# A recurrent memory transformer beside a routed expert: what is kept of each streamed weight block in SBUF

## The chip, the cores and the metric

The kernel runs on one core of one Trainium2 chip. The metric is the device time of one execution in microseconds. A core has a matrix engine (TensorE, PE in the profile, with its weight loads as PEld), VectorE (DVE), ScalarE (ACT), GpSimd (POOL), a sequencer that mostly issues DMAs (SyncE, SP), and sixteen DMA engines between HBM and the on-chip memory SBUF. Matmuls write to a second on-chip memory, PSUM.

## The reference

`x` is [2048, 1024] in bf16. It is normalised row by row; the result goes into two branches, and their sum and `x` are the output.

```
xn = layernorm(x)
out = x + A(xn) + B(xn)

# A: 64 segments of 32 rows, one after the other; 32 heads of 128, M = 8 memory rows
mem = mem0
for s in range(64):
    h = concat([mem, xn[32*s : 32*s+32]])          # 40 rows
    q, k, v = h @ Wq, h @ Wk, h @ Wv               # 1024 -> 32 heads x 128, each
    p = softmax(mask(q @ k.T * 128**-0.5))         # per head
    o = (p @ v) @ Wo                               # 4096 -> 1024
    mem = o[:8]
    outs.append(o[8:])

# B: the two rows with the largest xn @ w_r go through one gated expert
y = silu(xs @ w_gate) * (xs @ w_up) @ w_down       # 1024 -> 3584 -> 1024
B = xn, with y * sigmoid(r) added to the two rows
```

The memory rows of a segment come out of the segment before it, so the 64 segments run in sequence. Each one multiplies 40 rows by the four matrices Wq, Wk, Wv and Wo, 4 x 1024 x 4096 weights in bf16, 32 MB. SBUF does not hold all of that.

## The kernel before

**Granules.** The 32 MB of weights are cut into 64 granules of 128 x 2048 bf16: 512 KB, 4 KB in each of the 128 partitions. Granules 0 to 47 belong to Wq, Wk and Wv in the order of `PHASES` (six phases p of eight granules, kc = 0 to 7, each for half of the heads of one matrix); granules 48 to 63 belong to Wo, two heads each. A step is one segment and uses the granules in the order 0 to 63. One granule is four matmuls of 32 rows by 512 columns in the phases (L669, one for each quarter of 512 columns of the granule, into four partition groups of the accumulator `PSm`), and eight matmuls of 256 columns in the output projection (L730, into `WO`).

**Resident and streamed.** `streamed` (L75) lists 20 of the 64 granules, about every third; the other 44 are resident: loaded in the first step into a tile of their own (`load_resident`, L121, tiles `wres`) and kept. The streamed ones are loaded again in every step. In the first step they come from the input matrices, and GpSimd copies them once into contiguous DRAM tiles `wsc` (`copy_block`, L357), from which steps 1 to 63 read them (`fetch`, L327, issued by SP). They land in a pool of `N_SLOT` = 5 slots of 4 KB per partition (tile `g`). `after(s, g)` (L434) calls `fetch` whenever a streamed granule has been used, four granules ahead; in time, a load is issued when the matmuls of the granule that had its slot, five loads earlier, are done. SP issues its DMAs in program order.

**Two granules with other homes.** Granule 6 (`KEPT_WHOLE`) is held in PSUM, turned and turned back by `keep` (L334) in the first step, and brought into SBUF by `bring_back` (L348) in each later step: no load. Granule 25 (`KEPT_PART`) keeps its last two quarters in PSUM and streams the first two (`columns`, L107); `kept_piece` (L352) copies the two quarters from PSUM into the slot on VectorE in phase 2, after kc 1 and kc 2. So a step after the first has 19 loads, 18 of 512 KB and one of 256 KB.

**The rest of a step.** Small work is hung on places (p, kc) by `hook`: transposes of q and k (L516, copies QT on ACT and KT on DVE at kc 3 of the next phase), `scores` (L534, L536), `exponent` and `soften`, `attend` (L584, L586). A step ends with the cast of `WO` into `XN` (L791), whose memory rows feed the next step through two transposes (L259) and a copy into `ST` (L283). The memory rows' own outputs other than the recurrent ones ("left" rows, `left_pass` L647 into `PSl`, and `project` into `WL`) are computed for four segments together with the same granules while these are there. `after` also loads resident granules in the first step, 14 granules ahead, the last ten of them (whose tiles hold `x` before) from granule 44 on.

**The expert.** Its weights are 32 tiles of gate and up (448 KB each) and 14 of down (512 KB). In the last step `after` collects the tiles of used resident granules in `free_homes`, and `fetch_moe` (L371) loads into them; after the last step the five slots are added (L815), and all 46 loads have a place. Then come the choice of the two rows, 448 matmuls on gate and up (L873) and 112 on down (L886).

Of the kernel before, what the change touches and what calls it, by code (L numbers as in the profile page):

```python
# [8 lines left out]
BF16 = mybir.dt.bfloat16  # L9
# [5 lines left out]
PSUM = bass.MemoryType.PSUM  # L15
DRAM = bass.MemoryType.DRAM

N_RES = 44
N_SLOT = 5
KEPT_WHOLE = 6  # L20
KEPT_PART = 25
NEG = -30000.0

PHASES = [(0, 0), (1, 0), (0, 1), (1, 1), (2, 0), (2, 1)]
# [3 lines left out]
def kernel(  # L28
# [16 lines left out]
    nc = tc.nc  # L45
    P = 128
    Bsz, S, D = A_x.shape
# [7 lines left out]
    NT = S // P  # L55
# [16 lines left out]

    NG = 64

    streamed = [2, 5, KEPT_WHOLE, 9, 13, 17, 21, KEPT_PART, 29, 33, 36, 39, 42, 45, 47, 50, 53, 56, 59, 62]  # L75
    assert len(streamed) == NG - N_RES
    n_str = len(streamed)
    resident = [g for g in range(NG) if g not in streamed]

    def granule_dram(g):  # L80
        if g < 48:
            p, kc = divmod(g, KC)
            mat, half = PHASES[p]
            return Wqkv[mat][kc * P:(kc + 1) * P, 2048 * half:2048 * (half + 1)]
        w = g - 48
        return Wo2[2 * w * P:(2 * w + 2) * P, :].rearrange("(hh e) d -> e hh d", hh=2)

    def granule_out(t, g):
        return t[:, :] if g < 48 else t.rearrange("p (hh d) -> p hh d", hh=2)

    wres = ctx.enter_context(tc.tile_pool(name="wres", bufs=1))
    const = ctx.enter_context(tc.tile_pool(name="const", bufs=1))
    dram = ctx.enter_context(tc.tile_pool(name="dram", bufs=1, space=DRAM))
    front = ctx.enter_context(tc.tile_pool(name="front", bufs=1, reuse_waits="tile"))
    wstream = ctx.enter_context(tc.tile_pool(name="wstream", bufs=N_SLOT))
    one = ctx.enter_context(tc.tile_pool(name="one", bufs=1, reuse_waits="tile"))
# [7 lines left out]
    ql_d = [dram.tile([4, P, 512], BF16, name=f"ql_d{t}") for t in range(NT)]  # L104


    def columns(g, s):  # L107
        if s > 0 and g == KEPT_WHOLE:
            return None
        return slice(0, 1024 if s > 0 and g == KEPT_PART else 2048)  # L110

    wsc = {g: dram.tile([P, columns(g, 1).stop - columns(g, 1).start], BF16, name=f"wsc{g}")
           for g in streamed if g != KEPT_WHOLE}
    r_d = dram.tile([1, S], BF16, name="r_d")

# [2 lines left out]
    def home(g, shape, dtype, name):  # L118
        return wres.tile(shape, dtype, name=name, tag=f"wres{g}")
# [50 lines left out]
    for s in range(4):  # L170
        nc.vector.tensor_copy(out=SELM[:, s, 0:XM, :],
                              in_=IDENT[:, 32 * s:32 * s + XM].unsqueeze(2).to_broadcast([P, XM, 4]))
        nc.vector.tensor_copy(out=SELL[:, s, :, :],
                              in_=IDENT[:, 32 * s + XM:32 * s + SEG].unsqueeze(2).to_broadcast([P, XL, 4]))
# [129 lines left out]
    def new_stl(t):  # L304
# [7 lines left out]
    queued = []  # L312

    KEPT = [psK.tile([P, 1024], BF16, name=f"KEPT{b}") for b in range(3)]
    KEPT_COLS = {KEPT_WHOLE: {0: KEPT[0][:, 0:512], 1: KEPT[0][:, 512:1024], 2: KEPT[1][:, 0:512], 3: KEPT[1][:, 512:1024]},
                 KEPT_PART: {2: KEPT[2][:, 0:512], 3: KEPT[2][:, 512:1024]}}

    def fetch():
        if not flow:
            return  # L320
        s, g = flow.pop(0)
        t = wstream.tile([P, 2048], BF16, tag="g", name="g")
        c = columns(g, s)
        if s == 0:
            nc.sync.dma_start(out=granule_out(t, g), in_=granule_dram(g))
        elif c is not None:
            nc.sync.dma_start(out=t[:, c], in_=wsc[g][:, :])  # L327
        queued.append((g, t))

    def part(t, jq):  # L330
        return t[jq][:, :] if isinstance(t, list) else t[:, 512 * jq:512 * (jq + 1)]


    def keep(g, t):  # L334
        for c, K in KEPT_COLS[g].items():
            turned = PTB.rearrange("p (i r) -> p i r", i=4)
            for i in range(4):
                nc.tensor.transpose(out=turned[:, i, :], in_=t[:, 512 * c + P * i:512 * c + P * (i + 1)],
                                    identity=IDENT[:, :])
            XK = one.tile([P, 512], BF16, tag="vl", name="XK")  # L340
            nc.vector.tensor_copy(out=XK[:, :], in_=PTB)
            for i in range(4):
                nc.tensor.transpose(out=K[:, P * i:P * (i + 1)], in_=XK[:, P * i:P * (i + 1)], identity=IDENT[:, :])
# [7 lines left out]

    def kept_piece(g, c, copy):  # L352
        t = [t for q, t in queued if q == g][0]
        copy(out=t[:, 512 * c:512 * (c + 1)], in_=KEPT_COLS[g][c])  # L354


    def copy_block(g):  # L357
        c = columns(g, 1)
        if c is not None:
            src = granule_dram(g)  # L360
            nc.gpsimd.dma_start(out=granule_out(wsc[g], g), in_=src if g >= 48 else src[:, c])

    to_copy = list(streamed)
    flow += [(s, g) for s in range(NSEG) for g in streamed if s == 0 or g != KEPT_WHOLE]
# [1 line left out]
    moe = [("gu", w, kc, fh) for w in range(2) for kc in range(KC) for fh in range(2)]  # L366
    moe += [("dn", fg) for fg in range(FC // 2)]
    moe_tiles = {}
    free_homes = []

    def fetch_moe():  # L371
        while moe and free_homes:
            what = moe.pop(0)
            h = free_homes.pop(0)
            t = home(h, [P, 2048], BF16, "MW") if h >= 0 else wstream.tile([P, 2048], BF16, tag="g", name="g")
            if what[0] == "gu":
                _, w, kc, fh = what
                nc.sync.dma_start(out=t[:, 0:FH],
                                  in_=(B_w_gate, B_w_up)[w][kc * P:(kc + 1) * P, FH * fh:FH * (fh + 1)])
            else:  # L380
                nc.sync.dma_start(out=t.rearrange("p (a d) -> p a d", a=2),
                                  in_=B_w_down[2 * what[1] * P:(2 * what[1] + 2) * P, :].rearrange("(a p) d -> p a d", a=2))
            moe_tiles[what] = t

    def granule(g):
        if g in res_tiles:
# [28 lines left out]
    todo_res = [g for g in resident if g not in res_tiles]  # L415
# [18 lines left out]
    def after(s, g):  # L434

        if s == 0:
            if g in side:
                side[g]()
            if g % 2 == 1 and g >= 8 and to_copy:
                copy_block(to_copy.pop(0))  # L440
            if n_x_left and g % 2 == 1:
                load_x(n_x_left.pop(0))
            while todo_res and todo_res[0] <= g + 2 * 64 // n_str + 8 and (todo_res[0] < resident[-10] or g >= 2 * NT + 12):
                load_resident(todo_res.pop(0))
        if g in streamed and (s == 0 or g != KEPT_WHOLE):
            fetch()
        if s == NSEG - 1:
            if g in resident:
                free_homes.append(g)
            if not flow:  # L450
                fetch_moe()
# [49 lines left out]
    for s in range(NSEG):  # L501
# [8 lines left out]
        def hook(p, kc, fn):  # L510
            hooks.setdefault((p, kc), []).append(fn)
# [112 lines left out]
        if s > 0:  # L624
            hook(0, 0, lambda: bring_back(3, nc.scalar.copy))
            if j in (2, 3):
                hook(0, 1, lambda: bring_back(0, nc.vector.tensor_copy))
            hook(2, 1, lambda: kept_piece(KEPT_PART, 2, nc.vector.tensor_copy))
            hook(2, 2, lambda: kept_piece(KEPT_PART, 3, nc.vector.tensor_copy))
            hook(1, 5, turn_lx)  # L630
        hook(2, 6, lambda: scores(0))
        hook(3, 4, exponent)
# [93 lines left out]
        def project(PS, w, Gv, lhs, last):  # L726
            for hs in range(2):
                h = 2 * w + hs
                for g in range(4):
                    nc.tensor.matmul(PS[32 * g:32 * g + 32, 0:256], lhsT=lhs(h),  # L730
                                     rhs=Gv[:, D * hs + 256 * g:D * hs + 256 * (g + 1)], start=False,
                                     stop=(last and hs == 1), tile_position=(0, 32 * g), skip_group_check=True)

        def lhs_main(h):
# [77 lines left out]
        fn()  # L812


    free_homes += [-1] * N_SLOT  # L815
    fetch_moe()
    assert not moe
    T0 = one.tile([P, 1024], BF16, tag="vl", name="T0")
    XS = T0[0:2, :]
    T1 = one.tile([P, 1024], BF16, tag="otl", name="T1")  # L820
# [46 lines left out]
    for w in range(2):  # L867
        for kc in range(KC):
            for fh in range(2):
                Gt = moe_tiles["gu", w, kc, fh]  # L870
                for fl in range(FC // 2):
                    col = (w * FC + fh * (FC // 2) + fl) * 2
                    nc.tensor.matmul(GU[:, col:col + 2], lhsT=Gt[:, fl * P:(fl + 1) * P], rhs=XSELT[:, kc, :],  # L873
                                     start=(w + kc + fh + fl == 0), stop=True, skip_group_check=True)
    SG = T2[:, 64:64 + 4 * FC].bitcast(F32)
    nc.scalar.activation(out=SG, in_=GU[:, 0:FC * 2], func=ACTF.Silu)
    HT = T2[:, 256:256 + 2 * FC].rearrange("p (f c) -> p f c", c=2)
# [1 line left out]
    YP = psA.tile([P, 512], F32, tag="acc", name="YP")  # L879
    nc.vector.memset(YP[:, 0:256], 0.0)  # L880
    for fg in range(FC // 2):
        Gt = moe_tiles["dn", fg]
        for a in range(2):
            fc = 2 * fg + a
            for g in range(4):
                nc.tensor.matmul(YP[32 * g:32 * g + 2, 0:256], lhsT=HT[:, fc, :],  # L886
                                 rhs=Gt[:, a * D + 256 * g:a * D + 256 * (g + 1)], start=(fc == 0), stop=(fc == FC - 1),
                                 tile_position=(0, 32 * g))
# [39 lines left out]
```

## Time and profile before

| | us |
|---|---|
| median of three runs | 1912.75 |
| lowest and highest | 1907.44, 1921.95 |
| the profiled execution | 1914.95 |
| its span, first to last instruction | 1913.2 |

A page of the profile gives, for each engine, the time in which it was busy and what ended its idle time; DMA share is the mean busy share of the sixteen DMA engines. In rows of groups, `out<-in` names what an instruction writes and reads: `PSm<-g,ST` is a matmul into PSm on a streamed granule, `PSm<-wres,ST` on a resident one, `g<-wsc` a streamed load. Rows of windows give each engine's busy time in a stretch, then TensorE's granted clock, the DMA share and GB/s. Rows of waits give the total, the times and the longest. Behind `DMA to landing` stand the shortest, the median and the longest time from issue to landing.

### The profile page before, as it was taken

The numbers are of one execution on the slowest core, as the hardware profiler recorded it, in microseconds if no ns is written. First come the engines' busy times: TensorE is split into PE (matmuls) and PEld (weight loads), VectorE is DVE, ScalarE is ACT, GpSimd is POOL, SyncE is SP. The second block draws the span as 40 slices with busy tenths as digits, with TensorE's granted clock in tenths as the row PEclk, the third lists the DMA queues.
The fourth block names the chain that finished last, engine by engine and source line by source line (L and its number), as shares of the span: only waits on it lengthen the run. The fifth ranks groups of instructions, "written<-read, shape, count | busy, mean of one in ns | idle before, by whom it ended". The sixth has DMA issues, their size and how long they took to land. (4 is left out here: it accounts for less than half of the span.)

```text
span 1913.2 us, 82718 instructions
## 1 busy us (share of the span) xinstructions
PE 1607.9 (84%) x36320; PEld 891.0 (47%) x36320; DVE 906.8 (47%) x2884; ACT 703.0 (37%) x1886; POOL 294.0 (15%) x590
## 2 busy tenths in 40 slices
PE   3558898888889888989889898989888898889864
PEld 1224545444454445545454554545454544545443
DVE  6824544554455445444554454445444544455430
ACT  1113433443334343434344343334333443343320
POOL 2201111111110211112111111211121111111110
PEclk8669999999999999999999999999999999999995
DMA  9999999999999999999999999999999999999998
GB/s 369 399 363 378 358 381 365 380 379 354 383 352 390 350 382 376 378 381 369 387 353 373 370 372 362 362 387 365 370 363 384 376 366 385 365 386 368 393 390 330
DMA packets 224441, 712.39 MB, mean 372 GB/s; under 512 B 33664, under 2 KB 44464, under 8 KB 224080
## 3 DMA queue, kind: packets, MB, share of 16 engines
q1 hardware_dynamic: 194384, 671.18, 92.9%
q0 software_dynamic: 21056, 28.07, 4.4%
q10 hardware_dynamic: 8640, 7.87, 1.2%
q8 instruction: 283, 4.64, 0.9%
q14 instruction: 78, 0.64, 0.1%
HBM read 694.32 MB, written 22.29 MB: 375 GB/s over the span
## 5 line engine op out<-in xcount | busy, mean ns | idle before, releaser
L669 PE MATMUL PSm<-wres,ST 128*32 128x512 bf16 x8448 | 720.2, 385 | 21.2 <-DVE ST L283 6.7
L669 PEld LDWEIGHTS <-ST 128*32 128x32 bf16 x12288 | 325.8, 96 | 396.4 <-issue 166.9
L669 PE MATMUL PSm<-g,ST 128*32 128x512 bf16 x3588 | 362.4, 387 | 88.5 <-DMA g<-wsc 60.3
L685 ACT CAST XB<-PSm 128x512 bf16<-128x512 f32 x256 | 150.0, 586 | 306.9 <-PE PSm L669 305.3
L730 PEld LDWEIGHTS <-OT 128*32 128x32 bf16 x8192 | 214.1, 97 | 104.1 <-issue 80.8
L730 PE MATMUL WO<-wres,OT 128*32 128x256 bf16 x5632 | 237.2, 275 | 14.0 <-issue 8.9
L647 PE MATMUL PSl<-wres,STL 128*32 128x512 bf16 x2112 | 200.3, 390 | 1.5 <-issue 1.4
L526 DVE COPY KT<-BT 128x512 bf16<-128x512 bf16 x128 | 52.5, 410 | 307.7 <-ACT XB L685 148.9
L458 POOL DMA_DIRECT2D LX<-ql_d x63 | 33.8, 537 | 937.6 <-ACT OTL L593 525.0
L730 PE MATMUL WO<-g,OT 128*32 128x256 bf16 x2560 | 131.2, 279 | 54.4 <-DMA g<-wsc 42.0
L793 POOL DMA_DIRECT2D out_dram<-XN x256 | 129.6, 514 | 228.0 <-DVE XN L791 219.1
L707 ACT CAST VM<-PSm 128x512 bf16<-128x512 f32 x128 | 77.0, 602 | 153.5 <-PE PSm L669 121.5
L350 ACT COPY BK<-KEPT 128x512 bf16<-128x512 bf16 x126 | 78.3, 621 | 96.9 <-PE WO L730 96.9
L521 ACT COPY QT<-BT 128x512 bf16<-128x512 bf16 x128 | 75.0, 586 | 105.3 <-PE BT L516 99.7
L647 PEld LDWEIGHTS <-STL 128*32 128x32 bf16 x3072 | 85.1, 98 | 57.7 <-issue 8.0
L584 PEld LDWEIGHTS <-VM 32*128 32x128 bf16 x2048 | 67.6, 91 | 93.0 <-issue 71.3
L516 PEld LDWEIGHTS <-XB 128*128 128x128 bf16 x1024 | 58.5, 98 | 106.1 <-ACT XB L685 76.7
L543 DVE TENSOR_TENSOR BS<-BS,CT 128x96 f32<-128x96 f32 (+1 forms) x256 | 59.7, 233 | 100.8 <-PE BS L536 96.3
L354 DVE COPY g<-KEPT 128x512 bf16<-128x512 bf16 x126 | 47.6, 420 | 122.5 <-PE PSm L669 70.2
L791 DVE CAST XN<-WO 128x256 bf16<-128x256 f32 x64 | 27.2, 425 | 160.7 <-PE WO L730 160.7
L516 PE MATMUL BT<-IDENT,XB 128*128 128x128 bf16 x1024 | 102.0, 222 | 1.4 <-ACT QKL L476 1.4
L558 DVE TENSOR_REDUCE DN<-BS 128x8 f32<-128x320 f32 x128 | 63.0, 492 | 67.2 <-ACT BS L553 67.2
(168 smaller groups left out, 2382.2 us busy)
## 6 DMA issues: line engine op xcount, KB each, us to landing
g<-wsc SPq DMA_DIRECT2D x1134, 512.0 KB, 6.1
g<-wsc SPq DMA_DIRECT2D x63, 256.0 KB, 5.5
LX<-ql_d POOLq DMA_DIRECT2D x63, 128.0 KB, 6.0
ql_d<-XBl ACTq DMA_DIRECT2D x60, 128.0 KB, 5.6
MW<-in_B_w_gate_dram SPq DMA_DIRECT2D x16, 448.0 KB, 9.2
MW<-in_B_w_up_dram SPq DMA_DIRECT2D x16, 448.0 KB, 9.1
wres<-in_A_Wk_dram SPq DMA_DIRECT2D x12, 512.0 KB, 14.3
MW<-in_B_w_down_dram SPq DMA_DIRECT2D x12, 512.0 KB, 10.2
```

The lines of the kernel that those rows point to most:

```text
L350: copy(out=back[c][:, :], in_=KEPT_COLS[KEPT_WHOLE][c])
L516: nc.tensor.transpose(out=PTq[:, il, :, :].rearrange("p j r -> p (j r)"), in_=XB[:, il * P:(il + 1) * P], identity=IDENT[:, :])
L521: nc.scalar.copy(out=QT[half][:, :, :], in_=pv)
L543: nc.vector.tensor_tensor(out=S4, in0=S4, in1=m, op=ALU.add)
L558: nc.vector.tensor_reduce(out=DN[:, :], in_=S8, axis=AX.X, op=ALU.add)
L584: nc.tensor.matmul(o, lhsT=VM[half][q0:q0 + 32, il * P:(il + 1) * P], rhs=PTm[q0:q0 + 32, il, 0:NK], start=True, stop=False, tile_position ...
L647: nc.tensor.matmul(PSl[32 * jq:32 * jq + 32, :], lhsT=STL[:, g % KC, :], rhs=part(Gv, jq), start=first_, stop=last_, tile_position=(0, 32 ...
L669: nc.tensor.matmul(PSm[32 * jq:32 * jq + 32, :], lhsT=ST[:, kc, :], rhs=part(Gv, jq), start=(kc == 0), stop=(kc == KC - 1), tile_position= ...
L685: nc.scalar.copy(out=XB[:, :], in_=PSm[:, :])
L707: nc.scalar.copy(out=VM[half][:, :], in_=PSm[:, :])
L730: nc.tensor.matmul(PS[32 * g:32 * g + 32, 0:256], lhsT=lhs(h), rhs=Gv[:, D * hs + 256 * g:D * hs + 256 * (g + 1)], start=False, stop=(last ...
L793: nc.gpsimd.dma_start(out=out2[s * SEG:s * SEG + XM, 256 * g:256 * (g + 1)], in_=OB[32 * g:32 * g + XM, :])
```

## The change

The list of streamed granules grows from 20 to 25, and 39 remain resident in whole. Of each streamed granule the first quarter (512 columns, 1 KB per partition) stays in SBUF in a tile of its own, loaded in the first step; the three other quarters stream, so that a slot has 3 KB per partition. Exceptions: granule 6 still lies whole in PSUM; granule 62 keeps two quarters in SBUF; granules 23 and 26 (`KEPT_PARTS`) keep their last quarter in PSUM, one each in the place of the two quarters of granule 25. A step after the first has 24 loads, 21 of 384 KB and three of 256 KB. SBUF use is the same: 44 x 4 + 5 x 4 = 196 KB per partition before, 39 x 4 + 25 + 5 x 3 = 196 KB after (23 granules with one quarter, one with two).

A streamed granule is now handed on as a list of four quarters, and `part` and the new `span` pick out of it. In the first step a granule of Wo comes in up to three DMAs, since a row of it is two pieces of 2 KB. The expert's loads no longer use the slots: the last seven of 46 wait until matmuls on gate tiles free their tiles.

```diff
-N_RES = 44
 N_SLOT = 5
 KEPT_WHOLE = 6
-KEPT_PART = 25
+KEPT_PARTS = (23, 26)
+HALF_HOME = 62
...
-    streamed = [2, 5, KEPT_WHOLE, 9, 13, 17, 21, KEPT_PART, 29, 33, 36, 39, 42, 45, 47, 50, 53, 56, 59, 62]
+    streamed = [2, 5, KEPT_WHOLE, 8, 11, 14, 17, 20, 23, 26, 29, 32, 35, 37, 39, 41, 43, 45, 47, 50, 53, 55, 57, 60, 62]
...
+    def quarters_at_home(g):
+        return 0 if g == KEPT_WHOLE else 2 if g == HALF_HOME else 1
+
+    def travels(g, s):
+        if s > 0 and g == KEPT_WHOLE:
+            return None
+        return max(1, quarters_at_home(g)), 3 if s > 0 and g in KEPT_PARTS else 4
...
+    def move_columns(eng, t, g, lo, hi):
+        if g < 48:
+            eng.dma_start(out=t, in_=granule_dram(g)[:, lo:hi])
+            return
+        for hh in range(2):
+            a, b = max(lo, D * hh), min(hi, D * (hh + 1))
+            if a < b:
+                eng.dma_start(out=t[:, a - lo:b - lo], in_=granule_dram(g)[:, hh, a - D * hh:b - D * hh])
...
     def fetch():
...
-        t = wstream.tile([P, 2048], BF16, tag="g", name="g")
-        c = columns(g, s)
         if s == 0:
-            nc.sync.dma_start(out=granule_out(t, g), in_=granule_dram(g))
-        elif c is not None:
-            nc.sync.dma_start(out=t[:, c], in_=wsc[g][:, :])
-        queued.append((g, t))
+            for q in range(quarters_at_home(g)):
+                h = wres.tile([P, 512], BF16, name=f"quarter{g}_{q}", tag=f"quarter{g}_{q}")
+                move_columns(nc.sync, h[:, :], g, 512 * q, 512 * (q + 1))
+                at_home.setdefault(g, []).append(h[:, :])
...
+        t = wstream.tile([P, 1536], BF16, tag="g", name="g")
+        lo, hi = travels(g, s)
+        if s == 0:
+            move_columns(nc.sync, t[:, 512 * (lo - 1):512 * (hi - 1)], g, 512 * lo, 512 * hi)
+        else:
+            nc.sync.dma_start(out=t[:, 512 * (lo - 1):512 * (hi - 1)], in_=wsc[g][:, :])
+        home_q = at_home[g] if g in at_home else first_quarter
+        queued.append((g, home_q + [t[:, 512 * (q - 1):512 * q] for q in range(lo, 4)]))
...
+    def span(t, c0, n):
+        return t[c0 // 512][:, c0 % 512:c0 % 512 + n] if isinstance(t, list) else t[:, c0:c0 + n]
...
-            t = home(h, [P, 2048], BF16, "MW") if h >= 0 else wstream.tile([P, 2048], BF16, tag="g", name="g")
+            t = home(h, [P, 2048], BF16, "MW")
...
-            while todo_res and todo_res[0] <= g + 2 * 64 // n_str + 8 and (todo_res[0] < resident[-10] or g >= 2 * NT + 12):
+            while todo_res and todo_res[0] <= g + 14 and (todo_res[0] < resident[-10] or g >= 2 * NT + 12):
...
-            hook(2, 1, lambda: kept_piece(KEPT_PART, 2, nc.vector.tensor_copy))
-            hook(2, 2, lambda: kept_piece(KEPT_PART, 3, nc.vector.tensor_copy))
+            hook(2, 1, lambda: kept_piece(KEPT_PARTS[0], 3, nc.vector.tensor_copy))
+            hook(2, 2, lambda: kept_piece(KEPT_PARTS[1], 3, nc.vector.tensor_copy))
...
-                                     rhs=Gv[:, D * hs + 256 * g:D * hs + 256 * (g + 1)], start=False,
+                                     rhs=span(Gv, D * hs + 256 * g, 256), start=False,
...
-    free_homes += [-1] * N_SLOT
     fetch_moe()
-    assert not moe
...
-                Gt = moe_tiles["gu", w, kc, fh]
+                Gt, h = moe_tiles["gu", w, kc, fh]
...
+                free_homes.append(h)
+                fetch_moe()
+    assert not moe
```

More of the change, by code (lines that the diff above doesn't have):

```diff
@@ L73 @@
     NG = 64
-    streamed = [2, 5, KEPT_WHOLE, 9, 13, 17, 21, KEPT_PART, 29, 33, 36, 39, 42, 45, 47, 50, 53, 56, 59, 62]
-    assert len(streamed) == NG - N_RES
+    streamed = [2, 5, KEPT_WHOLE, 8, 11, 14, 17, 20, 23, 26, 29, 32, 35, 37, 39, 41, 43, 45, 47, 50, 53, 55, 57, 60, 62]
     n_str = len(streamed)
     resident = [g for g in range(NG) if g not in streamed]
+    def quarters_at_home(g):
[4 more added lines that the diff above has]
+        return max(1, quarters_at_home(g)), 3 if s > 0 and g in KEPT_PARTS else 4
     def granule_dram(g):
@@ L104 @@
     ql_d = [dram.tile([4, P, 512], BF16, name=f"ql_d{t}") for t in range(NT)]
[L107 to L112, printed above, removed]
+    wsc = {g: dram.tile([P, 512 * (travels(g, 1)[1] - travels(g, 1)[0])], BF16, name=f"wsc{g}")
            for g in streamed if g != KEPT_WHOLE}
@@ L315 @@
     KEPT_COLS = {KEPT_WHOLE: {0: KEPT[0][:, 0:512], 1: KEPT[0][:, 512:1024], 2: KEPT[1][:, 0:512], 3: KEPT[1][:, 512:1024]},
-                 KEPT_PART: {2: KEPT[2][:, 0:512], 3: KEPT[2][:, 512:1024]}}
+                 KEPT_PARTS[0]: {3: KEPT[2][:, 0:512]}, KEPT_PARTS[1]: {3: KEPT[2][:, 512:1024]}}
+    at_home = {}
     def fetch():
@@ L321, in fetch @@
         s, g = flow.pop(0)
-        t = wstream.tile([P, 2048], BF16, tag="g", name="g")
-        c = columns(g, s)
         if s == 0:
-            nc.sync.dma_start(out=granule_out(t, g), in_=granule_dram(g))
-        elif c is not None:
-            nc.sync.dma_start(out=t[:, c], in_=wsc[g][:, :])
-        queued.append((g, t))
+            for q in range(quarters_at_home(g)):
+                h = wres.tile([P, 512], BF16, name=f"quarter{g}_{q}", tag=f"quarter{g}_{q}")
+                move_columns(nc.sync, h[:, :], g, 512 * q, 512 * (q + 1))
+                at_home.setdefault(g, []).append(h[:, :])
+            if g == KEPT_WHOLE:
+                h = one.tile([P, 512], BF16, tag="bx", name="FIRST")
+                move_columns(nc.sync, h[:, :], g, 0, 512)
+                first_quarter.append(h[:, :])
+        t = wstream.tile([P, 1536], BF16, tag="g", name="g")
[6 more added lines that the diff above has]
+        queued.append((g, home_q + [t[:, 512 * (q - 1):512 * q] for q in range(lo, 4)]))
+    first_quarter = []
     def part(t, jq):
         return t[jq][:, :] if isinstance(t, list) else t[:, 512 * jq:512 * (jq + 1)]
+    def span(t, c0, n):
+        return t[c0 // 512][:, c0 % 512:c0 % 512 + n] if isinstance(t, list) else t[:, c0:c0 + n]
     def keep(g, t):
@@ L337, in keep @@
             for i in range(4):
-                nc.tensor.transpose(out=turned[:, i, :], in_=t[:, 512 * c + P * i:512 * c + P * (i + 1)],
+                nc.tensor.transpose(out=turned[:, i, :], in_=part(t, c)[:, P * i:P * (i + 1)],
                                     identity=IDENT[:, :])
@@ L353, in kept_piece @@
         t = [t for q, t in queued if q == g][0]
-        copy(out=t[:, 512 * c:512 * (c + 1)], in_=KEPT_COLS[g][c])
+        copy(out=t[c], in_=KEPT_COLS[g][c])
     def copy_block(g):
-        c = columns(g, 1)
+        c = travels(g, 1)
         if c is not None:
-            src = granule_dram(g)
-            nc.gpsimd.dma_start(out=granule_out(wsc[g], g), in_=src if g >= 48 else src[:, c])
+            move_columns(nc.gpsimd, wsc[g], g, 512 * c[0], 512 * c[1])
     to_copy = list(streamed)
@@ L382, in fetch_moe @@
                                   in_=B_w_down[2 * what[1] * P:(2 * what[1] + 2) * P, :].rearrange("(a p) d -> p a d", a=2))
-            moe_tiles[what] = t
+            moe_tiles[what] = t, h
     def granule(g):
@@ L881 @@
     for fg in range(FC // 2):
-        Gt = moe_tiles["dn", fg]
+        Gt = moe_tiles["dn", fg][0]
         for a in range(2):
```

## The prediction

> **What bounds the kernel now.** I read the stages first, then the DMA queues inside the long stage, then one step cut into quarters, then the waits. Three windows cut the span at the first and the last cast of L791, which ends each step:
>
> ```profile
> L791 DVE CAST XN<-WO x64: 424/425/426, 129.5 to 1851.7; 128x256 bf16<-128x256 f32 x64
> core 0: us, PE busy (x) PEld busy (x) DVE busy (x) ACT busy (x) POOL busy (x), PEclk, DMA share, GB/s
> 0.00:129.50 129.50, 58.55 (x745) 25.79 (x745) 76.96 (x189) 17.39 (x43) 21.80 (x49) 0.71 1.01 389
> 129.50:1851.80 1722.30, 1525.76 (x34930) 847.24 (x34934) 825.47 (x2680) 680.72 (x1836) 265.60 (x529) 0.99 1.00 372
> 1851.80:1913.20 61.40, 23.61 (x656) 17.96 (x645) 4.39 (x17) 4.85 (x7) 6.60 (x12) 0.57 0.90 346
> ```
>
> The 63 steps after the first take 1722.2 us, 27.34 us each: 90% of the span, with the sixteen DMA engines at share 1.00 and TensorE busy 89%. Two resources are nearly full at once. One step, from cast to cast, in quarters, shows that they take turns:
>
> ```profile
> 924.90:931.70 6.80, 6.20 (x102) 2.53 (x98) 1.67 (x5) 2.15 (x4) 2.59 (x6) 1.00 1.03 395
> 931.70:938.50 6.80, 6.80 (x148) 3.28 (x141) 3.46 (x11) 3.66 (x8) 0.53 (x1) 1.00 0.98 345
> 938.50:945.30 6.80, 6.54 (x177) 3.91 (x178) 5.40 (x17) 2.76 (x11) 0.00 (x0) 1.00 1.02 405
> 945.30:952.10 6.80, 4.24 (x134) 2.92 (x123) 2.74 (x12) 2.66 (x8) 0.54 (x1) 1.00 1.03 411
> ```
>
> In the second quarter TensorE is busy for all of its 6.80 us and the DMAs move 345 GB/s: there the slots are full and the loads wait for TensorE. In the last quarter the DMAs move 411 GB/s and TensorE is busy for 4.24 us of 6.80: there TensorE waits for loads. The waits and the matmul groups of the long stage put a size on it:
>
> ```profile
> PE PSm L669 <- DMA g<-wsc: 60.3, 125, 1.3
> PE WO L730 <- DMA g<-wsc: 42.0, 104, 1.2
> L669 PE MATMUL PSm<-wres,ST 128*32 128x512 bf16 x8316 | 703.0, 383 | 7.8 <-DVE ST L283 6.7 <-issue 1.1
> L669 PE MATMUL PSm<-g,ST 128*32 128x512 bf16 x3528 | 354.4, 385 | 65.8 <-DMA g<-wsc 60.3
> L730 PE MATMUL WO<-wres,OT 128*32 128x256 bf16 x5544 | 230.6, 273 | 9.1 <-issue 8.9
> L730 PE MATMUL WO<-g,OT 128*32 128x256 bf16 x2520 | 128.1, 277 | 48.1 <-DMA g<-wsc 42.0 <-issue 0.9
> ```
>
> TensorE stands idle 102.3 us for streamed weights. More is hidden in the busy time: a matmul on a resident granule costs 703.0/8316 = 84.5 ns, on a streamed one 354.4/3528 = 100.5 ns, because a group of four that starts after a wait does not overlap the group before it; on L730 it is 41.6 against 50.8 ns. That is 16.0 ns x 3528 + 9.2 ns x 2520 = 80 us. So all that late loads can cost is about 182 us.
>
> **The change: the loads of a step.** The price of a row comes from the queues of the long stage:
>
> ```profile
> q1 hardware_dynamic: 172246, 610.55, 94.0%
> q10 hardware_dynamic: 8640, 7.87, 1.3%
> g<-wsc SPq DMA_DIRECT2D x1129, 512.0 KB, 6.1
> g<-wsc SPq DMA_DIRECT2D x63, 256.0 KB, 5.5
> ql_d<-XBl ACTq DMA_DIRECT2D x60, 128.0 KB, 5.6
> ```
>
> q1 is nearly all rows of 4 KB: 0.940 x 16 x 1722.3 us / 610.55 MB = 42.4 ns per thousand bytes, 173.8 ns for a 4 KB row. q10 carries the 128 KB stores, rows of 1 KB: 0.013 x 16 x 1722.3 / 7.87 MB gives 46.6 ns a row (44.7 to 48.4 within the rounding of 1.3%). The line through both is 4.2 ns + 42.4 ns per KB: 131.4 ns for 3 KB and 89.0 ns for 2 KB. A load has 128 rows, eight per engine. Before, a step has 18 loads of 4 KB rows and one of 2 KB rows: 18 x 8 x 173.8 + 8 x 89.0 ns = 25.74 us per engine. After, it has 24 loads: 21 of three quarters (3 KB rows) and three of two quarters, granules 23, 26 and 62: 21 x 8 x 131.4 + 24 x 89.0 ns = 24.21 us. Five more loads add a completion packet per engine each; no row prices one, so it lies between the intercept of 4.2 ns and a 1 KB row of 46.6 ns, 0.02 to 0.23 us a step, taken as 0.1 as it carries no row. That leaves 1.43 us less DMA work a step (1.30 to 1.51), in 63 steps 90 us (82 to 95). In bytes it is 9.70 MB a step down to 9.04 MB, 6.8%; smaller rows give back about a sixth of that.
>
> How much of the 90 us is on the path? In the quarter in which TensorE is full, saved DMA work shortens nothing; if the saving is spread evenly, a quarter is lost: 68 us. But the new list puts its two short granules 23 and 26 into that quarter and its denser loads elsewhere, with three granules between loads in place of four, so the traffic there stays about 2.1 MB in 18 granules (0.117 MB per granule) against 2.36 MB in 20 (0.118 MB), and nearly all of the saving falls into the stretches that wait for DMA: 90 us. I take the middle, **79 us**.
>
> **The cover.** Five slots stay, but each holds 3 KB a partition. A slot's cycle is now 5 x 27.34/19 = 7.19 us: 6.1 us from issue to landing and 1.1 us until it is issued again. After, with steps of 26.1 us, it is 5 x 26.1/24 = 5.44 us, so a load may take 4.3 us to land. The quickest landing bounds what it needs:
>
> ```profile
> L327 SPq DMA_DIRECT2D g<-wsc x1197: 319/320/1107, 118.8 to 1845.1; - x200
> DMA to landing us min/median/max: 3.2/6.1/14.7
> ```
>
> 4.3 us is above 3.2 us, so the DMA engines keep 1.1 us of queue where they had 2.9 us. That is thinner, but a queue that does not run dry costs nothing; its price if it does is the second rival. Issuing is no limit: 24 x 0.32 us = 7.7 us of a step on SP.
>
> On this cover the Trainium skill speaks against the change: "DMA: Bandwidth & Descriptors", section "Rules for kernel authors", asks for at least 1 MiB per DMA, and its section on the anatomy of one DMA gives a fixed cost of about 2.0 us per DMA plus bytes at 436 GB/s. By that a load of 512 KB takes an estimated 3.2 us and one of 384 KB 2.9 us, and a step's loads taken one after another would go from 60 to 69 us, 14% more. The trace disagrees with paying that fixed part once per load: 19 loads take 27.34 us, 1.44 us each, because five overlap.
>
> **The small parts, at nothing.** TensorE gets the same matmuls; a matmul on a home quarter reads a tile that was loaded in the first step. The first matmul of a streamed granule no longer waits for its load, the second does; nothing is gained by that, since the other three still wait. The copies from PSUM into slots (L354) are now for two granules instead of one, and each waits for its own slot's last user, granules 8 and 11 in place of 5; VectorE reaches them in phase 2, six granules after 11, and behind them stands the copy KT that TensorE needs at phase 2, kc 3:
>
> ```profile
> DVE g L354 <- PE PSm L669: 70.2, 38, 2.9
> PE BS L534 <- DVE KT L526: 9.5, 17, 0.6
> ```
>
> TensorE loses 9.5 us in all to KT; if the cover of six granules were gone it would be some such sum again. In the first step the copies into DRAM shrink by the same 0.66 MB, 1.7 us at 389 GB/s, and 25 home quarters come as 1 KB rows at 46.6 ns in place of a quarter of 173.8 ns, 25 x 8 x 3.2 ns = 0.6 us, with some 30 more DMAs queued on SP; granule 48 is loaded later (at granule 44, since it is now one of the last ten residents), at most one wait of a few us. I take 0, between -3 and +4 us.
>
> In the tail 46 expert loads had 44 homes and two slots; now they have 39, and the last seven wait on SP until gate matmuls free homes:
>
> ```profile
> 1845.78 15.20 SPq L378 DMA_DIRECT2D MW<-in_B_w_gate_dram  x16
> 1880.23 14.05 SPq L381 DMA_DIRECT2D MW<-in_B_w_down_dram  x12
> 1870.81 4.80 PE L873 MATMUL GU<-T,MW 128*128 128x2 bf16 x174
> ```
>
> By 1875.6 the gate matmuls have used twelve tiles (174 of 14 each), and the 40th load is issued near 1880.23 + 7 x 1.17 = 1888. The homes are free 12 us earlier: 0, and if that cover went, seven loads at 1.2 us, 8 us. On SP only the last two stores stand behind them.
>
> **The sum.** The profiled execution took 1914.95 us (span 1913.2), 2.2 us above the median of the three runs. 1914.95 - 79 = 1836; with the median 1834. I forecast **1835 us**, and 1810 to 1865 for this case: the lower end is the full 95 us of DMA work and 10 us of the 80 us hidden in streamed matmuls, the upper end about half of the work lost to a queue that at times runs dry.
>
> **The rivals.** *More than the bytes.* TensorE and DMA are both near full, and the two lose time by taking turns; with 24 evenly spread loads the waits could mostly go; the DMAs have room for that, since at the 411 GB/s of the last quarter a step's bytes would need less time than the mean of 372 GB/s shows. The whole 102 us of idle gives 1813 us, the whole 182 us gives 1733; I price it at two thirds of 182, 1794 us. For it: loads spaced by two to three granules. Against it: the second quarter shows TensorE full at 6.80, which no load shortens.
>
> *The lookahead decides, and it is slower.* If a load's landing time is mostly fixed, not queue, then smaller loads in the same five slots move fewer bytes per cycle. The two landing rows, 6.1 us for 512 KB and 5.5 us for 256 KB, taken as they stand give 5.8 us for 384 KB; a cycle of 6.9 us, 24/5 cycles a step, 33.1 us: +365 us, 2280 us. It decides from a landing of 27.34 x 5/24 - 1.1 = 4.6 us on; at 5.0 us the step is 29.3 us and the time 2037 us; a landing of 4.8 us gives 1975 us. The skill's fixed 2.0 us per DMA is this rival's rule; its 14% on a step would be an estimated 2156 us. Against it: 5 slots x 6.1/7.19 = 4.2 loads are in flight, and 4.2 x 1.43 us (25.74 us over 18 full loads) is 6.0 us, so the landing time is just the queue at a full share of 1.00; and the quickest load took 3.2 us.
>
> *Nothing comes out.* Landing about 4.6 us, or the saved work falls where TensorE is full: 1895 to 1930 us, within 1% either way, 1910 us. That the loads are not what the diff says can be left out: the built program issues 24 of them in each of 63 steps.
>
> **Chances.** Forecast 0.57, more than the bytes 0.18, nothing 0.12, slower 0.13. A difference under 1% (19 us; the three runs spread over 14.5 us) can't be told from none: faster than 1894 us has 0.75, within 1% 0.11, slower 0.14. The range 1785 to 1885 us takes in the forecast case, nearly all of the first rival and a little of the third: 0.57 + 0.16 + 0.04 = 0.77, about 8 in 10.
>
> **What would show it.** Step length 26.1 us from cast to cast (L791). Landing of the three-quarter loads at 4.3 us: at 4.6 or more the second rival has begun. q1 should carry 41 MB less in the long stage, 569 MB, with its share still at 90% or more. TensorE's waits for g should fall from 102.3 us to some 60 us, and the price of a streamed matmul from 100.5 towards 84.5 ns. The second quarter should keep TensorE full and its length; the last should shrink most. The forecast is wrong if GB/s in the long stage drops below 355 (it should be 360 to 372) or if TensorE waits elsewhere, for KT or in the first step.

## The result, and the profile after

| | us |
|---|---|
| before, median of four runs | 1913.9 |
| changed, median of four runs (2018.51 to 2027.91) | 2021.85 |
| ratio, with its 95% interval | 1.0565 (1.0517 to 1.0613) |
| span of the profiled execution, before and changed | 1913.2, 2019.3 |

The change makes the kernel 5.65% slower. The forecast was 1835 us, with a range from 1785 to 1885 us.

The casts that end the steps, and the three windows that they cut, in the changed kernel (columns: us; busy time and instructions of PE, PEld, DVE, ACT and POOL; TensorE's granted clock; DMA share; GB/s):

```profile
L816 DVE CAST XN<-WO x64: 423/425/426, 133.4 to 1957.1; 128x256 bf16<-128x256 f32 x64
```

```profile
0.00:133.40 133.40, 67.93 (x745) 27.78 (x745) 76.96 (x188) 17.30 (x43) 25.89 (x59) 0.67 1.00 367
133.40:1957.20 1823.80, 1599.38 (x34933) 854.33 (x34934) 833.91 (x2680) 680.39 (x1836) 265.04 (x529) 0.99 0.96 329
1957.20:2019.30 62.10, 24.68 (x645) 19.54 (x641) 4.38 (x17) 4.85 (x7) 6.58 (x12) 0.55 0.89 343
```

Of the 106.1 us between the two spans, 101.5 lie in the 63 steps (1823.7 against 1722.2 us, 28.95 against 27.34 us a step), 3.9 in the first step, the rest in the tail. In the steps the DMAs move 329 GB/s where they moved 372. The queue that carries the loads, and the loads, in that window (packets, MB, share of 16 engines; then us from issue to landing):

```profile
q1 hardware_dynamic: 217725, 570.00, 89.6%
...
g<-wsc SPq DMA_DIRECT2D x1318, 384.0 KB, 5.2
g<-wsc SPq DMA_DIRECT2D x189, 256.0 KB, 4.5
```

The bytes fell as the diff says, from 610.55 to 570.00 MB. The landing did not fall to 4.3 us, it stands at 5.2. A step in quarters shows where the rate went:

```profile
944.90:952.10 7.20, 6.78 (x118) 3.19 (x114) 1.44 (x4) 3.09 (x6) 2.57 (x6) 1.00 0.97 339
952.10:959.40 7.30, 5.90 (x125) 2.76 (x118) 4.18 (x12) 2.69 (x6) 0.17 (x1) 1.00 0.98 320
959.40:966.60 7.20, 6.67 (x155) 3.42 (x157) 4.23 (x13) 2.84 (x11) 0.00 (x0) 1.00 0.96 326
966.60:973.90 7.30, 5.70 (x167) 3.61 (x158) 2.88 (x12) 2.27 (x7) 0.53 (x1) 1.00 0.98 362
```

Before, the DMAs reached 405 and 411 GB/s in the two last quarters, in which TensorE was not full, and fell to 345 in the quarter in which it was. Now TensorE is full in no quarter (5.90 of 7.30 us in the second), and the DMAs reach 362 GB/s at best. Neither resource is at its limit, although the DMA share still says 0.96 to 0.98. TensorE's waits in the steps, and its groups on resident and streamed granules:

```profile
PE PSm L694 <- DMA g<-wsc: 113.7, 189, 2.4
PE WO L755 <- DMA g<-wsc: 44.3, 68, 1.7
```

```profile
L694 PE MATMUL PSm<-wres,ST 128*32 128x512 bf16 x7308 | 691.6, 382 | 7.1 <-DVE ST L294 6.7 <-issue 0.4
L694 PE MATMUL PSm<-g,ST 128*32 128x512 bf16 x3402 | 451.5, 385 | 120.7 <-DMA g<-wsc 113.7
L694 PE MATMUL PSm<-quarter,ST 128*32 128x512 bf16 x1134 | 435.6, 384 | 0.0
```

Idle time for loads is 158.0 us where it was 102.3. The groups can no longer be priced per matmul as before: the home quarter's matmul (`PSm<-quarter`) is a group of its own with one matmul per granule, 384 ns each, which in time overlaps the three others, so its 435.6 us are mostly the same microseconds as those of `PSm<-g`.

### The profile page after: what moved, and what is told of

It reads as the page before. It is cut to its first block, busy times and chain, and to the rows that moved or that the text cites. A ratio compares the mean times of both kernels' runs of the same rounds, so it can differ in the third digit from the quotient of the medians.

```text
span 2019.3 us, 83566 instructions
## 1 busy us (share of the span) xinstructions
PE 1692.0 (84%) x36320; PEld 901.7 (45%) x36320; DVE 915.2 (45%) x2884; ACT 702.5 (35%) x1886; POOL 297.5 (15%) x600
## 5 line engine op out<-in xcount | busy, mean ns | idle before, releaser
L694 PE MATMUL PSm<-wres,ST 128*32 128x512 bf16 x7424 | 708.4, 384 | 7.1 <-DVE ST L294 6.7
L694 PEld LDWEIGHTS <-ST 128*32 128x32 bf16 x12288 | 353.6, 96 | 522.9 <-issue 306.0
L694 PE MATMUL PSm<-g,ST 128*32 128x512 bf16 x3459 | 462.2, 388 | 130.7 <-DMA g<-wsc 113.7
L694 PE MATMUL PSm<-quarter,ST 128*32 128x512 bf16 x1152 | 445.2, 386 | 16.3 <-DMA quarter<-in_A_Wk_dram 10.4
L755 PE MATMUL WO<-wres,OT 128*32 128x256 bf16 x5120 | 253.8, 277 | 11.0 <-DMA wres<-in_A_Wo_dram 7.6
L755 PE MATMUL WO<-g,OT 128*32 128x256 bf16 x2176 | 147.5, 278 | 49.1 <-DMA g<-wsc 44.3
L672 PEld LDWEIGHTS <-STL 128*32 128x32 bf16 x3072 | 96.9, 98 | 51.3 <-issue 8.0
L672 PE MATMUL PSl<-g,STL 128*32 128x512 bf16 x867 | 118.3, 394 | 0.0
L755 PE MATMUL WO<-quarter,OT 128*32 128x256 bf16 x896 | 114.1, 277 | 4.7 <-DMA quarter<-in_A_Wo_dram 4.6
L672 PE MATMUL PSl<-quarter,STL 128*32 128x512 bf16 x288 | 114.3, 397 | 0.0
```

The costliest lines, as they stand in the source:

```text
L672: nc.tensor.matmul(PSl[32 * jq:32 * jq + 32, :], lhsT=STL[:, g % KC, :], rhs=part(Gv, jq), start=first_, stop=last_, tile_position=(0, 32 ...
L694: nc.tensor.matmul(PSm[32 * jq:32 * jq + 32, :], lhsT=ST[:, kc, :], rhs=part(Gv, jq), start=(kc == 0), stop=(kc == KC - 1), tile_position= ...
```

## The experiments

**Three theories.** *Depth*: five slots of 3 KB hold too few bytes in flight, the DMA engines run short of queued work, and the rate falls. *Loads or rows*: 24 loads in place of 19, or rows of 3 KB in place of 4 KB, cost DMA time by themselves. *Schedule*: the places of the loads, the copies on VectorE, or the group of four matmuls that now begins with a home quarter.

**The rate by itself.** A kernel that leaves out the whole computation and only streams, in stages; a slot is loaded again as soon as its load has landed. It ran once, as did the second streaming kernel further down.

```diff
+    def stage(cols, slots, n, pitch=0):
+        pitch = pitch or cols
+        with tc.tile_pool(name=f"r{cols}_{slots}_{pitch}", bufs=slots) as pool:
+            for k in range(n):
+                t = pool.tile([P, cols], BF16, tag="g", name="g")
+                at = (k % (n_max // (P * pitch))) * P * pitch
+                nc.sync.dma_start(out=t[:, :], in_=flat[at:at + P * pitch].rearrange("(p c) -> p c", c=pitch)[:, 0:cols])
```

> A kernel that leaves out the whole computation and only streams Wo into SBUF, in fourteen stages: rows of 4, 3 or 2 KB, 3 to 8 slots, each load issued when the load that had its slot has landed; one stage of 3 KB rows at a pitch of 4 KB. Depth theory: the rate is set by the bytes in flight until it saturates near 400 GB/s; 5 slots of 3 KB lie clearly below 5 slots of 4 KB, and 6 or 7 slots of 3 KB reach the rate of 5 slots of 4 KB; 4 slots of 4 KB lie near 5 slots of 3 KB. Row theory: 3 KB rows stay 5 to 15% below 4 KB rows however many slots there are, and the pitch of 4 KB changes that.

Windows inside the stages (us, POOL busy, granted clock, DMA share, GB/s). In order: 4 KB rows with 3, 4, 5, 6 and 8 slots; 3 KB rows with 3, 4, 5, 6, 7 and 8; 3 KB rows at a pitch of 4 KB with 5; 2 KB rows with 5 and 8:

```profile
26.90:74.50 47.60, 0.00 (x0) 1.00 0.90 319
90.30:128.30 38.00, 0.00 (x0) 1.00 1.03 410
144.10:181.20 37.10, 0.00 (x0) 1.00 1.03 411
196.60:233.70 37.10, 0.00 (x0) 1.00 1.03 411
247.90:285.00 37.10, 0.00 (x0) 1.00 1.03 411
307.00:357.10 50.10, 0.00 (x0) 1.00 0.93 305
371.40:417.70 46.30, 0.00 (x0) 1.00 0.97 335
431.10:469.70 38.60, 0.00 (x0) 1.00 1.03 397
482.90:521.10 38.20, 0.00 (x0) 1.00 1.03 403
534.50:572.70 38.20, 0.00 (x0) 1.00 1.03 403
584.50:623.40 38.90, 0.00 (x0) 1.00 1.03 403
641.20:681.80 40.60, 0.00 (x0) 1.00 1.00 373
694.80:743.30 48.50, 0.00 (x0) 1.00 0.94 316
752.20:792.30 40.10, 0.00 (x0) 1.00 1.05 386
```

With enough slots, 3 KB rows reach 403 GB/s against 411: the shorter row costs 2%, not 5 to 15%. What sets the rate below that is how much is in flight. Three slots of 3 KB, 1.18 MB, give 305 GB/s; 1.57 MB give 319 (three slots of 4 KB) and 335 (four of 3 KB); 1.97 MB give 397 (five of 3 KB) and 2.10 MB give 410 (four of 4 KB). So much for rows of 3 KB as the cause; rows of 2 KB stay at 386 with 2.10 MB in flight. The depth theory's statement that five slots of 3 KB lie clearly below five of 4 KB did not hold here, 397 against 411: without TensorE, five slots of 3 KB are just enough. In the kernel they give 329. A pitch of 4 KB does not make the rate higher (373), so the packed rows of `wsc` are not the trouble.

**Fewer slots before, more slots after.**

```diff
 before_4slots
-N_SLOT = 5
+N_SLOT = 4
 after_6slots (after_7slots: seven, and 55, 60, 47 share the quarters of 20, 29, 32 as well)
-N_SLOT = 5
+N_SLOT = 6
+SHARED = {50: 11, 53: 14, 57: 17}
...
             for q in range(quarters_at_home(g)):
+                if g in SHARED:
+                    at_home[g] = at_home[SHARED[g]][:1]
+                    continue
```

> The kernel before with four slots instead of five: the same 19 loads of 4 KB rows, less in flight. Depth theory: four slots hold 2.10 MB where five of 3 KB hold 1.97 and five of 4 KB 2.62; by a line through the two known rates (328 and 372 GB/s in the steps) 337 GB/s, steps of 30.1 us, about 2090 us. Load-count or row theory: nothing is added, 1915 to 1930 us. Schedule theory (the places of the loads, the copies on VectorE, the order of the matmuls): 1915 to 1940 us.

> The changed kernel with six slots of 3 KB; the room comes from three streamed granules (50, 53, 57) that use the home quarter of another granule (11, 14, 17), so part of the weights is wrong; loads per step, rows and matmuls are the same 24, 3 KB and all. Depth theory: 2.36 MB of slots, about 354 GB/s, steps of 26.8 us, about 1890 us. Load-count or row theory and schedule theory: within 1% of the changed kernel, 2010 to 2030 us.

> The same with seven slots, six streamed granules sharing a home quarter. Depth theory: 2.75 MB of slots, DMA no longer short, steps of 25.5 to 26.1 us (what the forecast had), about 1835 us. Load-count or row theory and schedule theory: 2010 to 2030 us.

The six- and seven-slot kernels leave out three and six of the home quarters and use another granule's in their place, so they stand for the time alone. Measured: four slots before 2124.19 us, ratio to before 1.1067 (1.1027 to 1.1108); six slots after 1899.04 us, 0.9888 (0.9856 to 0.9921); seven slots after 1843.03 us, 0.9589 (0.9558 to 0.9619). The ratios are to runs of the kernel before beside these, with a median of 1921.42 us. The depth theory had said 2090, 1890 and 1835 us. One slot less, with nothing else changed, costs the kernel before more than the whole change did; one slot more takes the loss back. With four slots before, TensorE's waits for loads are three times the 102.3 us of five:

```profile
PE PSm L669 <- DMA g<-wsc: 177.7, 238, 3.6
PE WO L730 <- DMA g<-wsc: 131.6, 176, 2.6
```

TensorE's granted clock in these steps was 0.95 where it was 0.99 before, which explains little of it: a matmul of 512 columns took 392 ns in place of 383. In the changed kernel the same 24 loads of the same rows run at another rate with more slots, with fewer waits (the loads' landing and TensorE's waits, six slots, then seven; then the steps of the seven-slot kernel, with the columns of the three windows above):

```profile
g<-wsc SPq DMA_DIRECT2D x1323, 384.0 KB, 5.6
g<-wsc SPq DMA_DIRECT2D x189, 256.0 KB, 5.1
```

```profile
PE PSm L698 <- DMA g<-wsc: 58.6, 113, 1.9
...
PE WO L759 <- DMA g<-wsc: 5.6, 12, 1.1
```

```profile
g<-wsc SPq DMA_DIRECT2D x1323, 384.0 KB, 5.9
g<-wsc SPq DMA_DIRECT2D x189, 256.0 KB, 5.3
```

```profile
PE PSm L698 <- DMA g<-wsc: 11.0, 24, 1.2
...
PE WO L759 <- DMA g<-wsc: 1.6, 5, 0.4
```

```profile
129.60:1781.60 1652.00, 1513.33 (x34933) 841.18 (x34934) 830.85 (x2680) 678.78 (x1836) 265.64 (x529) 0.99 1.00 364
```

The landing time rises with each slot, 5.2, 5.6, 5.9 us, and yet the kernel gets faster: a longer landing here is a longer queue. The load-count and row theories fall, and the schedule theory with them as far as the places of the loads and the copies on VectorE go, since they are the same in the changed kernel with five, six and seven slots.

**The order of the four matmuls.**

```diff
-                for jq in range(4):
+                for jq in ((1, 2, 3, 0) if isinstance(Gv, list) else range(4)):
                     nc.tensor.matmul(PSm[32 * jq:32 * jq + 32, :], lhsT=ST[:, kc, :], rhs=part(Gv, jq),
```

> The changed kernel, with the home quarter's matmul as the last of the four of a streamed granule instead of the first, so that the four start together behind the wait. Depth theory: the wait is the same, 2010 to 2030 us. If splitting the group of four costs TensorE time (its busy time rose by 84 us): 1940 to 1990 us.

2029.33 us, ratio to before 1.0579 (1.0527 to 1.063), beside the 1.0565 of the change itself: no difference. TensorE's busy time over the span, 1607.9 us before and 1692.0 after, is 1663.2 with the home quarter last, and its waits for loads are 191.9 us in place of 158.0: a third of the larger busy time turned into waits, and the kernel took as long. A split group in itself takes no longer. In the seven-slot kernel, where loads are in time, groups with a home quarter start 0.22 us apart (at 900.45, 900.67 and 900.89 us in one step), as whole groups do before (912.04, 912.26 and 912.47 us).

**Does a slot count while its load has landed and stands?** In the streaming kernel a slot is loaded again at once; in the kernel it stands for a while: the cycle is 5 x 28.95/24 = 6.03 us, of which 5.2 is landing. The streaming kernel again, with 0, 1, 2 or 4 copies of the landed tile on VectorE before its slot is free:

```diff
+                for u in range(uses):
+                    nc.vector.tensor_copy(out=scratch[:, :], in_=t[:, 0:512])
```

> A kernel that leaves out the whole computation, as the depth curve did: stages of streamed loads, but a slot is given back only after 0, 1, 2 or 4 short copies on VectorE have read the landed tile, so that it stands landed for a while as it does under TensorE. If a slot counts only while its load is in flight: five slots of 3 KB fall from 397 GB/s with no copy to 330 to 350 with a hold near 0.9 us, six to about 395, seven stay at 400; five of 4 KB stay above 400 with the same hold and four of 4 KB fall from 410 to 345 to 370. If the hold does not matter, and something else in the kernel slows the loads: every stage keeps the rate of its stage without copies within 2%.

Five slots of 3 KB with 0, 1, 2 copies, then four of 4 KB with 0 and 4 copies, then five of 4 KB with 0 and 4 (us, DVE busy, POOL busy, clock, DMA share, GB/s):

```profile
21.90:61.70 39.80, 0.00 (x0) 0.00 (x0) 1.00 1.01 380
76.50:117.40 40.90, 11.47 (x39) 0.00 (x0) 1.00 1.00 371
133.00:176.40 43.40, 22.94 (x78) 0.00 (x0) 1.00 0.98 351
...
402.50:440.10 37.60, 0.00 (x0) 0.00 (x0) 1.00 1.02 409
460.70:506.80 46.10, 34.06 (x116) 0.00 (x0) 1.00 0.94 329
523.20:560.40 37.20, 0.00 (x0) 0.00 (x0) 1.00 1.03 410
580.00:619.00 39.00, 34.08 (x116) 0.00 (x0) 1.00 1.01 386
```

The hold matters. Five slots of 3 KB fall from 380 to 351 GB/s with two copies; a load then takes 393216 B / 351 GB/s = 1.12 us, a cycle 5.6 us, a landing 4.8 us, so the hold is 0.8 us. Four slots of 4 KB fall from 409 to 329 with a hold of 1.5 us (landing 4.9 us), below the 345 to 370 expected. In the three stages of 3 KB with four copies VectorE itself is busy 90% and sets the rate, so those say nothing, also not on what was expected of six and seven slots, and five slots of 4 KB at 386 are near that limit too. Two points stay uncertain: five slots of 3 KB without copies gave 380 GB/s here and 397 in the first curve, and the kernel's 329 is lower than the 351 of a like hold. Three of its 24 loads are only 256 KB, which makes the mean slot 368 KB, and its consumption is uneven; how the remaining difference divides was not tried.

**The exchange of slots for home.** All SBUF that streamed granules stop using in slots goes into weights at home, so the change exchanges 5 KB per partition of slot for 5 KB of home, 0.66 MB a step. Three kernels take other points of that exchange in the same SBUF, with no shared quarters:

```diff
 home38_6slots (home37_7slots: N_SLOT = 7, and 13, 16, 18, 21 in place of 14, 17, 20)
-N_SLOT = 5
+N_SLOT = 6
-    streamed = [2, 5, KEPT_WHOLE, 8, 11, 14, 17, 20, 23, 26, 29, 32, 35, 37, 39, 41, 43, 45, 47, 50, 53, 55, 57, 60, 62]
+    streamed = [2, 5, KEPT_WHOLE, 8, 11, 14, 17, 20, 23, 26, 28, 31, 33, 35, 37, 39, 41, 43, 45, 47, 50, 53, 55, 57, 60, 62]
 before43_6slots
-N_RES = 44
-N_SLOT = 5
+N_RES = 43
+N_SLOT = 6
-    streamed = [2, 5, KEPT_WHOLE, 9, 13, 17, 21, KEPT_PART, 29, 33, 36, 39, 42, 45, 47, 50, 53, 56, 59, 62]
+    streamed = [2, 5, KEPT_WHOLE, 9, 13, 17, 21, KEPT_PART, 28, 31, 34, 36, 39, 42, 45, 47, 50, 53, 56, 59, 62]
...
```

> The changed kernel at the same SBUF with one granule less at home in whole: 38 whole, 26 streamed with a quarter at home, six slots of 3 KB; 25 loads and 9.43 MB a step; the whole computation. If depth and bytes at home trade against each other: at the 351 GB/s that the steps had with six slots, steps of 28.2 us, 1950 to 1975 us, between the changed kernel and the one before. If the number of loads costs: slower than the changed kernel, 2030 us or more.

> The same with 37 whole, 27 streamed with a quarter at home, seven slots of 3 KB; 26 loads and 9.83 MB a step; the whole computation. Trade of depth against bytes: at 372 to 385 GB/s, steps of 26.8 to 27.7 us, 1880 to 1940 us, about the kernel before. Load-count theory: 2040 us or more.

> The kernel before with 43 granules at home and six slots of 4 KB; 20 loads and 10.2 MB a step; the whole computation. Trade of depth against bytes: depth is enough already, so the rate gains little (385 to 390 GB/s) and the bytes cost 0.3 to 1.4 us a step: 1930 to 2000 us. If depth alone mattered: faster than before, 1850 us.

Measured: 1968.69 us, ratio 1.0246 (1.0202 to 1.0291); 1929.84 us, 1.0061 (1.0031 to 1.009); 1916.29 us, 0.9982 (0.9952 to 1.0012), beside a median of 1916.41 us of the kernel before. The first two came as the exchange has it; the third was priced too high (1930 to 2000 us), it is level with the kernel before. All kernels in one table, by the KB of slots per partition, with the bytes of streamed loads a step and the mean GB/s over the span of the profiled execution:

| kernel | slots | KB of slots | MB a step | GB/s | us |
|---|---|---|---|---|---|
| changed | 5 x 3 KB | 15 | 9.04 | 332 | 2021.85 |
| before, four slots | 4 x 4 KB | 16 | 9.70 | 332 | 2124.19 |
| changed, six slots, shared quarters | 6 x 3 KB | 18 | 9.04 | 354 | 1899.04 |
| 38 at home, six slots | 6 x 3 KB | 18 | 9.44 | 354 | 1968.69 |
| before | 5 x 4 KB | 20 | 9.70 | 372 | 1913.9 |
| changed, seven slots, shared quarters | 7 x 3 KB | 21 | 9.04 | 364 | 1843.03 |
| 37 at home, seven slots | 7 x 3 KB | 21 | 9.83 | 375 | 1929.84 |
| before with 43 at home | 6 x 4 KB | 24 | 10.22 | 387 | 1916.29 |

The column of GB/s follows the column of slot KB, whatever the rows, the number of loads and the bytes. One row lies off, 364 at 21 KB: there the loads no longer set the pace (12.6 us of waits in all), and TensorE does, busy 92% of steps of 26.2 us. The two kernels that are faster than the one before have more room than there is, by the shared quarters; within the SBUF that there is, none of the four tried beats it.

## Why the prediction was wrong, point by point

**What bounds the kernel**: right. Two nearly full resources that take turns, 102 us of idle time for loads.

**The DMA work of a step**: right in bytes (570.00 MB against a forecast 569). The row price holds at depth: in the streaming kernel 403 against 411 GB/s is a row of 3 KB at 0.765 of one of 4 KB, where the line through 1 KB and 4 KB gave 131.4/173.8 = 0.756. It does not hold in the changed kernel. There the loads' queue has a share of 89.6% of 28.95 us, 25.9 us of work a step, where 24.3 us were forecast and the kernel before had 94.0% of 27.34 us, 25.7 us. The same bytes with seven slots:

```profile
q1 hardware_dynamic: 217804, 570.29, 93.6%
```

That is 24.5 us of 26.2, close to the forecast: a packet takes longer when less is in flight, so with five slots of 3 KB the saved work was not even there as work. The seven-slot kernel's 1843 us is close to the forecast 1835 as well, but in part by luck: it has more slot room than the kernel before (21 KB against 20), its waits for loads fell to 12.6 us where some 60 were forecast, and TensorE sets its pace.

**The cover**: this is the step that failed. It read: "4.3 us is above 3.2 us, so the DMA engines keep 1.1 us of queue where they had 2.9 us", and then, "a queue that does not run dry costs nothing". The 3.2 us is the landing of the quickest load of 1197. It says how soon one load can land, not how much has to be in flight for all sixteen engines to be full. The term was put at nothing, and the steps took 101.5 us more where they were to take 79 us less. The curve shows what is needed. The landings there, from its queues in the windows of three, four and five slots of 3 KB (305, 335 and 397 GB/s), then of three and four slots of 4 KB (319 and 410):

```profile
g<-in_A_Wo_dram SPq DMA_DIRECT2D x39, 384.0 KB, 3.8
```

```profile
g<-in_A_Wo_dram SPq DMA_DIRECT2D x40, 384.0 KB, 4.7
```

```profile
g<-in_A_Wo_dram SPq DMA_DIRECT2D x40, 384.0 KB, 4.9
```

```profile
g<-in_A_Wo_dram SPq DMA_DIRECT2D x30, 512.0 KB, 4.9
```

```profile
g<-in_A_Wo_dram SPq DMA_DIRECT2D x30, 512.0 KB, 5.1
```

All these landings are above 3.2 us, and yet only two of the five stages are near full rate; three slots of 4 KB land in 4.9 us at 319 GB/s, five of 3 KB in 4.9 us at 397. A landing above the quickest one is not yet a full queue. What tells the stages apart is the bytes: about 5 us x 400 GB/s = 2 MB must be in flight. Before, 5 slots x 499 KB x 6.1/7.19 are 2.2 MB in flight; after, 5 x 368 KB x 5.2/6.03 are 1.6 MB, and the curve has 319 to 335 GB/s for 1.57 MB. The kernel's 329 agrees. Such a product is the rate of the loads times their landing time, so it gives the size only; the cause is shown by the slots that were taken away and added with the loads unchanged. Why 1.6 MB in flight move no more than that stays open. The term was bounded from the wrong row: the landing rows of 6.1 and 5.5 us were at hand, and the prediction put them into a rival.

**The second rival** came nearest to what happened: it was to decide from a landing of 4.6 us on and gave 2037 us for 5.0 us; the landing is 5.2 us for the full loads (5.1 over all) and the time 2022 us. It had a chance of 0.13. Two of its terms were off. Its condition, a mostly fixed landing time, does not hold: the landing fell from 6.1 to 5.2 us, and with 5.8 us it gave 2280. And a landed slot stood for 0.8 us (6.03 - 5.2) where it took 1.1. What was set against it, that 4.2 loads in flight make up the landing time, could not decide: loads in flight times the time per load give the landing time whatever sets it, after the change as well (5 x 5.2/6.03 = 4.3 loads, 4.3 x 28.95/24 = 5.2 us). Its 1.43 us a load also divides the work of 18 full loads and a short one by 18.

On the fixed cost, the Trainium skill ("DMA: Bandwidth & Descriptors", the section on the anatomy of one DMA) gives about 2.0 us plus the bytes at 436 GB/s, fitted to DMAs that GpSimd issues; these loads are issued by SP. By it a load of 512 KB takes an estimated 3.2 us, and three such loads in flight would be more than enough for full rate. The trace does not agree: three slots of 512 KB give 319 GB/s with landings of 4.9 us. It pointed the right way, slower, but not to the size.

**Where the saving falls**: the argument about quarters has no object, as the rate fell in all four quarters, also in the one in which TensorE had been full (320 against 345).

**The small parts**: the first step cost 3.9 us (said: -3 to +4), the tail 0.7 (said: 0), and the order of the matmuls does nothing. The copies on VectorE do not delay KT; TensorE's wait for it fell from 9.5 us to 1.5.

**The tests**: the landing of "4.6 or more" (5.2) and GB/s "below 355" (329) told it; TensorE's waits for loads rose to 158.0 us in place of falling to some 60. The "share still at 90% or more" came out at 89.6% beside a rate 12% lower, so it tells little.

## What to carry to other kernels

SBUF serves a stream in two ways: weights kept at home need not be loaded, and slots hold the bytes in flight. Before moving room from slots to home, measure the rate by what is in flight, counting a slot only while its load travels (slots x size x landing / cycle). Here the exchange is worth nothing from 20 to 24 KB of slots and a loss below (2.5% at 18 KB, 5.7% at 15). A DMA share near 1.00 does not say that the DMAs are at their rate (here 0.97 stood beside 335 GB/s): look at GB/s in a stretch in which nothing else holds the loads.

## What the runs showed of the hardware

The DMA share hardly tells a short queue: it was 0.90 to 0.97 at 305 to 335 GB/s and 1.03 at 397 to 411. So a packet takes longer when the queue is shallow: with rows of 3 KB, an engine was busy 0.97 x 16/335 = 46.3 ns per thousand bytes with four slots and 1.03 x 16/403 = 40.9 ns with six. The landing time of a load rose with what was in flight before the rate was full, 3.8 us with three loads of 384 KB and 4.7 us with four, 4.9 us with three of 512 KB; the quickest load landed in 3.0 to 3.2 us in the two kernels. And 3 KB rows at a pitch of 4 KB came at 373 GB/s where packed ones came at 397 in the same run; packed ones gave 380 in the second streaming kernel, so the size of this difference is open.
